# A retention layer with a SwiGLU FFN: the FFN's products from three 12-bit products in two sums, in place of float32 products with Strassen's scheme

## The chip, the cores and the metric

The kernel runs on one NeuronCore of a Trainium2 chip. The metric is the device time of one execution in microseconds (us). Three executions of the kernel before took 707.82, 710.52 and 709.75 us; the median is 709.75 us. TensorE (PE in the profile, PEld for its weight loads) multiplies, VectorE (DVE) and ScalarE (ACT) work on SBUF and PSUM, GpSimd (POOL) works on SBUF alone, and SyncE (SP) issues most DMAs.

## The reference

The attention half is a decayed recurrence over 768 positions, for 4 sequences and 8 heads of 64. Its output, laid out as 3072 tokens of 512 values, goes through a SwiGLU block with a hidden width of 1536.

```python
gamma = 1.0 - 2.0 ** (-5.0 - np.arange(H))
for t in range(S):
    state = gamma * state + k[:, :, t] (x) v[:, :, t]      # outer product, per head
    y[:, :, t] = scale * q[:, :, t] @ state
x = y.transpose(0, 2, 1, 3).reshape(B * S, H * D)          # 3072 x 512
g = x @ w_gate                                             # 512 x 1536
silu = g * (1.0 / (1.0 + np.exp(-g)))
val = x @ w_val                                            # 512 x 1536
return (silu * val) @ w_out                                # 1536 x 512
```

The FFN's weights reach the kernel as float64 numbers, seen as pairs of 32-bit words.

## The kernel before, in words

**Retention.** The recurrence is done in chunks of 128 positions: scores of a chunk, times a mask of decays, times v, plus q times the state carried from the chunk before. `retention` (helpers at L502) does it for two sequences at a time with matmuls of 64 rows; the first segment has older forms (L385, L425, L442, L445). All of it is float32.

**Segments.** The 3072 tokens go through in 4 segments (NSEG) of 6 chunks, so 768 tokens, held as two halves of 384 (TH). A segment is a stage "up" (x times w_gate and w_val, gate, product) and a stage "down" (times w_out). While a segment's down stage runs, the retention matmuls of the next segment are placed between its products (`step`, called after each product, pops them from a list by a table of due places, DUE).

**Strassen.** Every FFN product is one level of Strassen's scheme in Winograd's form, 7 products for 8, and from the second segment on the up stage nests a second level (`up2`). Sums of weight blocks and of token blocks have to be made first: `sums_t` and `sums_u` for the weights, `sums_x`, `sums_2` and `sum_h` for the tokens; and the products have to be joined (L755, ACT, DVE and POOL). Weight sums of the second level, 21 units of 896 KB, are kept in DRAM and read again in each segment through a ring of 6 buffers (`load_unit`).

**The matmuls.** A float32 matmul of the source stands in the trace as two MATMUL records, each with a LDWEIGHTS record. The up stage of the first segment has 168 matmuls of 384 columns (L679), that of each later segment 294 of 192 columns (L790), a down stage 126 of 256 columns (L873 and L883).

**Conversion.** In the first up stage the weights are converted from float64 words to float32 by `convert_a` (ACT: absolute value at L237, sign into a PSUM bank at L241, low word at L244), `convert_b` (DVE: clamp at L254, shift at L256, sign merged at L260) and `convert_c` (POOL: integer add at L269). A block of w_gate with w_val is 128x1024, a block of w_out 128x512. DMAs: L215 for the words, L144 for the converted sums back to DRAM.

**Order.** All orders are written out by hand: every engine runs its instructions in the order in which the source issued them, and waits in that order. L114 loads chunks at the start; `load_side` (L476, L477) loads masks in pieces.

Of the kernel before, what the change touches and what calls it, by code (L numbers as in the profile page):

```python
# [10 lines left out]
F32 = mybir.dt.float32  # L11
I32 = mybir.dt.int32
# [12 lines left out]
L = 3  # L25
TH = L * P
NSEG = B * NCK // (2 * L)
KH = NC // 2
FH = NF // 2
DH = DM // 2  # L30
HT = TH // 2
NQ = NF // 4
NU = 7 * NQ
RING = 6
TA = 3 * P


MASK0, QDEC0, KDEC0, GDEC0 = 0, 2 * NP * P, 3 * NP * P, 3 * NP * P + H
NTAB = GDEC0 + NP


@with_exitstack
def tile_retnet_swiglu(
# [16 lines left out]

# [9 lines left out]
    def place(name, n):  # L90
        return consts.tile([P, n], F32, name=name)

    hsp, midp, loadp, iop = (place(nm, n) for nm, n in (
        ("hsp", 4 * FH * P), ("midp", 6 * TA), ("loadp", 8 * 512), ("iop", 6 * 512)))
    hT = consts.tile([P, NF, 2, TH], F32, name="hT")
    ring = [consts.tile([P, 7 * KH * P], F32, name=f"ring{i}") for i in range(RING)]
    banks = [psum.tile([P, 512], F32, name=f"bank{i}") for i in range(8)]
    turn = {}

    def bank(tag):  # L100


        own = {"s": (4, 5), "y": (6, 7)}[tag]
        turn[tag] = turn.get(tag, -1) + 1
        return banks[own[turn[tag] % len(own)]]


    chunks = {}

    def load_chunk(c, places):  # L110

        for t in places:
            own = chunks.setdefault(c, [])
            nc.sync.dma_start(out=t, in_=(k_t, q_t, v_n, k_n)[len(own)][c])  # L114
            own.append(t)

    def seg_chunks(s):

        p, pos = divmod(s * L, NCK)
        return [(2 * p + i) * NCK + pos + j for j in range(L) for i in range(2)]  # L120

    tab = consts.tile([P, NTAB], F32, name="tab")


    wt = {}
    wot = [consts.tile([P, 7, DH], F32, name=f"wot{j}") for j in range(FH)]
    T3, B22, B12, T1, B11, B21, T2, T4 = 0, 1, 2, 2, 3, 4, 5, 6


    U1, U11, U21, U3, U22, U2, U4 = range(7)  # L130
    unit_b = [kept.tile([P, 7, 2, 4, P], F32, name=f"unitb{q}", tag=f"unitb{q}")
              for q in range(NQ)]
    unit_t = [kept.tile([P, 2, 7, P], F32, name=f"unitt{n}", tag=f"unitt{n}")
              for n in range(NU)]
    PRODUCTS = (1, 5, 6, 2, 7, 3, 4)
    SLOT = {1: B11, 5: T1, 6: T2, 2: B21, 7: T3, 3: B22, 4: T4}

    def new_wt(f):
        wt[f] = ring[f % 4].rearrange("p (a b) -> p a b", a=7)

    def keep_wt(f):

        q, b, h = f // 4, f // 2 % 2, f % 2
        nc.sync.dma_start(out=unit_b[q][:, :, h, ds(2 * b, 2)],  # L144
                          in_=wt[f].rearrange("p a (k f) -> p a k f", k=KH))

    units = {}

    def load_unit(n, whole, slot=None):
        t = ring[n % RING if slot is None else slot]  # L150
        t = t.rearrange("p (h a b) -> p h a b", h=2, a=7)
        if whole:
            nc.sync.dma_start(out=t, in_=unit_t[n])
        else:
            nc.sync.dma_start(out=t[:, :, ds(U11, 4)],
                              in_=unit_b[n // 7][:, SLOT[PRODUCTS[n % 7]]])
        units[n] = t

    def sums_u(n, engine=nc.vector):

        w = units[n]
        sub = engine.tensor_tensor

        def first():
            sub(w[:, :, U1 : U3 + 1 : 3], w[:, :, ds(U3, 2)], w[:, :, U11 : U3 + 1 : 2],
                op=ALU.subtract)

        def last():
            sub(w[:, :, U4], w[:, :, U21], w[:, :, U2], op=ALU.subtract)  # L169
            nc.sync.dma_start(out=unit_t[n], in_=w)  # L170

        return [first,
                lambda: sub(w[:, :, U2], w[:, :, U22], w[:, :, U1], op=ALU.subtract),
                last]

    raw = {}

    def span(piece):  # L180

        kind, a, h = piece
        if kind == "up":
            return wt[a], B22, 4
        return wot[a], (B22, B11)[h], 2

    def load_piece(piece):

        kind, a, h = piece
        if kind == "up":  # L190
            new_wt(a)
            gate, val = (w[:, ts(a, P)].rearrange("(c p) f -> p c f", p=P)
                         for w in (w_gate, w_val))
            parts = [(val[:, ds(KH, KH)], 0), (val[:, ds(0, KH)], 1), (gate, 2)]
        else:
            top, low = (w_out[ts(a + FH * i, P)] for i in range(2))
            parts = ([(low[:, DH:], 0), (top[:, DH:], 1)],
                     [(top[:, :DH], 0), (low[:, :DH], 1)])[h]
        to, slot, n = span(piece)
        to = to[:, ds(slot, n)]  # L200
        if w_gate.dtype != F32:
            t = raw_places[kind].pop(0)
            if kind == "down" or a:
                raw_places[kind].append(t)
            to = raw[piece] = t.bitcast(U32).rearrange("p (a b) -> p a b", a=n)
        for src, i in parts:
            if w_gate.dtype != F32:
                src = src.bitcast(U32)
# [7 lines left out]

# [51 lines left out]
    def sums_t(piece, parts=range(3)):  # L274
# [10 lines left out]
        if kind == "up" and parts[-1] == 2:  # L285
            keep_wt(a)

# [861 lines left out]
```

## Time and profile before

| what | value |
|---|---|
| runs | 707.82, 709.75, 710.52 us |
| span of the profiled execution, first to last instruction | 706.6 us |
| own device time of the profiled execution | not given; the runs' median is 3.15 us over its span |
| granted TensorE clock | 1.000 of full speed |
| PE busy | 691.0 us, 5132 records |
| DVE, ACT, POOL busy | 466.0, 251.5, 240.2 us |
| DMA | 139.92 MB, mean 198 GB/s |

The profile is of one execution. Busy time is the time in which an engine has at least one instruction running; a group's "mean ns" is the length of one record, and PE's records overlap, so the time that a matmul costs is read from how many of them a stretch without gaps holds. "Chain" is the work that ended last, followed back from the last instruction; a stretch of it that says "PE bank L790 x584" is 584 records with nothing between them.

### The profile page before, as it was taken

The page shows a single profiled execution, that of the slowest core. Times are in us where ns is not written, and L with a number is a line of the kernel's source. Part 1 is how long each engine was busy: PE and PEld are TensorE (multiplying, and loading weights), DVE is VectorE, ACT ScalarE, POOL GpSimd, SP SyncE. Part 2 cuts the span into 40 slices and gives each one's busy share as a digit, 9 for nine tenths or more (in the row PEclk, how much of TensorE's full clock was granted, in tenths as well). Part 3 has the DMA queues.
Part 4 walks back from the last instruction along what each step waited for, and adds up shares of the span by engine and source line. Part 5 has one row for each costly group of instructions (what it writes and reads, how often), then busy time and mean ns, then how long its engine had stood idle before and what let it go on. Part 6 is the DMA issues. An engine that isn't in the chain of part 4 may idle for free.

```text
span 706.6 us, 12979 instructions
## 1 busy us (share of the span) xinstructions
PE 691.0 (98%) x5132; PEld 601.3 (85%) x5132; DVE 466.0 (66%) x830; ACT 251.5 (36%) x514; POOL 240.2 (34%) x147
## 2 busy tenths in 40 slices
PE   7998999999999899999999999999999999999998
PEld 7654555578888899998888999998888999999887
DVE  3887998778858987876353675657551666657420
ACT  2658777511333233421322333331222324342000
POOL 0334444403300738280230455474210182644000
PEclk9999999999999999999999999999999999999999
DMA  9798897657999858581570555562291255630010
GB/s 316 261 369 281 284 300 239 176 138 221 354 355 369 316 183 306 206 252 45 188 305 1 186 198 198 194 210 67 84 374 38 86 205 209 209 105 0 24 37 30
DMA packets 63356, 139.92 MB, mean 198 GB/s; under 512 B 6336, under 2 KB 30272, under 8 KB 63296
## 3 DMA queue, kind: packets, MB, share of 16 engines
q1 hardware_dynamic: 59552, 132.81, 55.6%
q10 hardware_dynamic: 3744, 6.29, 2.4%
q8 instruction: 40, 0.66, 0.4%
q14 instruction: 20, 0.16, 0.1%
HBM read 102.51 MB, written 36.57 MB: 197 GB/s over the span
## 4 chain that ended last, share of the span: by engine, by line
PE 83%; DMA 8%; DVE 3%; issue 3%; ACT 2%; POOL 1%; SPq 0%; DVEq 0%; ACTq 0%; POOLq 0%
PE bank L790 38%; PE bank L873 23%; PE bank L679 13%; PE bank L502 4%; PE bank L883 4%; DMA out_dram<-iop 1%; DMA unitt<-ring 1%; DMA loadp<-in_w_gate_dram 1%; DMA hsp<-in_w_gate_dram 1%; DMA hT<-in_v_n_dram 1%; DMA loadp<-in_q_t_dram 1%; DMA ring<-unitb 1%; DMA hT<-in_k_t_dram 1%; DVE ring L169 0%; DVE iop L755 0%
## 5 line engine op out<-in xcount | busy, mean ns | idle before, releaser
L790 PE MATMUL bank<-loadp,ring 128*128 128x192 f32 x720 | 140.6, 327 | 0.7 <-DVE iop L755 0.7
L873 PE MATMUL bank<-wot,hsp 128*128 128x256 f32 x576 | 129.4, 382 | 0.0
L790 PEld LDWEIGHTS bank<-loadp,ring 128*128 128x128 f32 x720 | 120.4, 190 | 2.4 <-DVE iop L755 1.3
L873 PEld LDWEIGHTS bank<-wot,hsp 128*128 128x128 f32 x576 | 108.1, 190 | 16.0 <-issue 1.4
L755 DVE TENSOR_TENSOR iop<-bank,iop 128x384 f32<-128x384 f32 x144 | 79.7, 556 | 50.1 <-PE bank L790 46.8
L790 PE MATMUL bank<-xs,ring 128*128 128x192 f32 x432 | 88.0, 326 | 1.2 <-DVE iop L755 1.2
L755 ACT COPY hsp<-bank 128x384 f32<-128x384 f32 x90 | 42.9, 478 | 102.5 <-PE bank L790 94.0
L825 POOL TENSOR_TENSOR hT<-iop 128x768 f32<-128x768 f32 x36 | 67.1, 1863 | 35.4 <-DVE iop L755 35.4
L755 POOL TENSOR_TENSOR iop<-hsp,midp 128x768 f32<-128x768 f32 x9 | 16.3, 1812 | 174.8 <-ACT hsp L755 140.3
L790 PEld LDWEIGHTS bank<-xs,ring 128*128 128x128 f32 x432 | 73.1, 190 | 1.5 <-DVE iop L755 1.5
L790 PE MATMUL bank<-xT,ring 128*128 128x192 f32 x324 | 66.3, 327 | 0.2 <-DVE midp L755 0.2
L873 PE MATMUL bank<-wot,hT 128*128 128x256 f32 (+1 forms) x300 | 65.9, 373 | 0.5 <-ACT iop L960 0.4
L679 PE MATMUL bank<-xs,ring 128*128 128x384 f32 x192 | 64.7, 488 | 1.1 <-ACT iop L700 0.5
L873 PEld LDWEIGHTS bank<-wot,hT 128*128 128x128 f32 x300 | 54.9, 190 | 8.4 <-DVE iop L948 0.6
L679 PEld LDWEIGHTS bank<-xs,ring 128*128 128x128 f32 x192 | 36.1, 190 | 27.8 <-ACT iop L700 1.1
L790 PE MATMUL bank<-hsp,ring 128*128 128x192 f32 x288 | 56.7, 326 | 0.5 <-ACT hsp L755 0.5
L790 PEld LDWEIGHTS bank<-xT,ring 128*128 128x128 f32 x324 | 54.7, 190 | 1.4 <-DVE iop L755 0.8
L755 DVE TENSOR_TENSOR midp<-bank,midp 128x384 f32<-128x384 f32 x72 | 39.9, 554 | 17.9 <-PE bank L790 14.8
L679 PE MATMUL bank<-xT,ring 128*128 128x384 f32 x144 | 49.8, 489 | 1.8 <-DVE hT L716 1.6
L790 PEld LDWEIGHTS bank<-hsp,ring 128*128 128x128 f32 x288 | 48.4, 190 | 0.8 <-ACT hsp L755 0.8
L944 DVE TENSOR_TENSOR iop<-bank,iop 128x256 f32<-128x256 f32 x12 | 5.1, 424 | 64.7 <-PE bank L873 51.8
L679 PEld LDWEIGHTS bank<-xT,ring 128*128 128x128 f32 x144 | 26.9, 190 | 21.9 <-DVE hT L716 2.2
(152 smaller groups left out, 973.4 us busy)
## 6 DMA issues: line engine op xcount, KB each, us to landing
ring<-unitt SPq DMA_DIRECT2D x50, 896.0 KB, 4.6
unitt<-ring SPq DMA_DIRECT2D x21, 896.0 KB, 6.0
unitb<-ring SPq DMA_DIRECT2D x12, 896.0 KB, 7.0
ring<-unitb SPq DMA_DIRECT2D x21, 512.0 KB, 5.9
out_dram<-iop ACTq DMA_DIRECT2D x23, 256.0 KB, 2.5
loadp<-in_w_val_dram SPq DMA_DIRECT2D x18, 256.0 KB, 4.1
loadp<-in_w_gate_dram SPq DMA_DIRECT2D x9, 512.0 KB, 6.6
midp<-in_w_out_dram SPq DMA_DIRECT2D x12, 256.0 KB, 6.0
```

The lines of the kernel that those rows point to most:

```text
L502: nc.tensor.matmul(o, a, b, start=start, stop=True, skip_group_check=True)
L679: nc.tensor.matmul(o, w[:, slot, k], a[:, k], start=(start and k == 0), stop=(stop and k == KH - 1), skip_group_check=True)
L755: events.append((t, len(events), lambda: fn(*args, **kw)))
L790: nc.tensor.matmul(o[:, h], w[:, h, slot], rhs, start=(start and h == 0), stop=True, skip_group_check=True)
L825: by_block(9.5, 13.5, lambda r: pool(to[:, r], u2[:, r], p5[:, r], op=add))
L873: nc.tensor.matmul(o[:, cols], a[:, k], wot[k][:, slot, cols], start=(start and k == 0), stop=(k == FH - 1), skip_group_check=True)
L883: nc.tensor.matmul(o, a_dn(0, 0, u)[:, k], wot[k][:, B11], start=(k == 0), stop=(k == FH - 1), skip_group_check=True)
L944: tt(ev[0][:, DH:], wb, u2, op=ALU.add)
```

## The change

The Strassen sums, their buffers, the ring of units and the DRAM copies of sums are gone. The kernel has 6 segments (NSEG = NCK) of 512 tokens: one chunk of all four sequences. The first segment's up products stay float32 matmuls, now 8 per block of 128 hidden columns with 512 columns each, straight (`up_first`). All other FFN products (5 up stages, 6 down stages) are made of three matmuls each on operands of the type float32r (R12 in the source), in which both operands have been cut to 12 significant bits: a value a becomes hi (a times CUT, stored as R12), lo (a minus hi) and mid (a combination of both), and the three products hi·hi, lo·lo and mid·mid go into two PSUM sums, that `bring` (ACT) and `joined` (DVE) put together. w_out is converted in the first up stage, split there into its three parts, and stays in SBUF; w_gate and w_val are converted there, kept in DRAM as float32 (512 KB per block, `keep_up`), and read and split again in every later segment (`load_raw`, `up_hi` on ACT, `up_lo` on POOL, `up_mid` on DVE). The hidden values are split in the same way (`h_hi`, `h_lo`, `h_mid`). The instruction order is no longer written as nested loops with places: every call is entered in a list with a planned time, `at(time, function)`, and the list is sorted by it; on each engine the order of the calls is what remains of these times.

The diff, cut to its core. Of the products:

```diff
-            def product(o, slot, rhs, start):                    # up2, 192 columns
-                w = units[n]
-                for h in range(2):
-                    nc.tensor.matmul(o[:, h], w[:, h, slot], rhs,
-                                     start=(start and h == 0), stop=True,
-                                     skip_group_check=True)
...
-            for k in range(FH):                                  # down, 256 columns
-                nc.tensor.matmul(o[:, cols], a[:, k], wot[k][:, slot, cols],
...
+TOK = B * P
+NSEG = NCK
...
+    def up_first(f, g, o):
+        for c in range(NC):
+            nc.tensor.matmul(banks[o], block(made[f % 4], g, c), xr[:, c], start=c == 0,
+                             stop=c == NC - 1, skip_group_check=True)
...
+    def up(x, f, g, part, o):
+        w = w_of[f]
+        for c in range(NC):
+            nc.tensor.matmul(banks[o + (part == 2)], block(w[:, part], g, c), x[:, part, c],
+                             start=c == 0 and part != 1, stop=c == NC - 1 and part != 0,
+                             skip_group_check=True)
...
+    def down(u, j, part, o):
+        h = h_of[u, j]
+        for k in range(FH):
+            nc.tensor.matmul(banks[o + (part == 2)], h[:, part, ts(k, P)],
+                             wo[part][:, FH * j + k],
+                             start=j == k == 0 and part != 1,
+                             stop=j == 1 and k == FH - 1 and part != 0,
+                             skip_group_check=True)
```

Of the splits and joins:

```diff
+    def hi_of(o, a):
+        nc.scalar.activation(o, a, AF.Copy, scale=CUT)
+    def lo_of(o, a, hi, op=pool):
+        op(o, a, f32(hi), op=sub)
+    def mid_of(o, lo, hi):
+        stt(o, f32(lo), -FAR, f32(hi), op0=mul, op1=add)
+    def wo_hi(i):
+        nc.vector.tensor_scalar(wo[0][:, i], down_made(i), CUT, None, op0=mul)
+    def wo_lo(i):
+        lo_of(wo[1][:, i], down_made(i), wo[0][:, i])
+    def wo_mid(i):
+        mid_of(wo[2][:, i], wo[1][:, i], wo[0][:, i])
+    def wo_far(i):
+        nc.gpsimd.tensor_scalar(wo[1][:, i], f32(wo[1][:, i]), FAR, None, op0=mul)
...
+    def bring(i, o):
+        nc.scalar.activation(outs[i], banks[o], AF.Copy, scale=BACK)
+    def joined(i, o, to=None):
+        stt(banks[o + 1] if to is None else to, banks[o + 1], CZ, outs[i], op0=mul, op1=add)
+    def up_gate(f, o):
+        nc.scalar.activation(sg(f), banks[o + 1], AF.Silu)
+    def up_val(f, o):
+        tt(hT[:, f], banks[o + 1], sg(f), op=mul)
```

Of the plan for the start and the first up stage (`convert_abs`, `convert_sign`, `convert_low` are ACT's three steps at 1024 or 512 columns, `convert_clamp`, `convert_shift`, `convert_merge` DVE's, `convert_add` POOL's):

```diff
+    PASS = 0.216
+    UP, HB = 24 * PASS, 18 * PASS
+    ORDER = [(0, 0), (1, 0), (0, 1), (1, 1), (2, 0), (2, 1), (3, 0), (3, 1)]
+    for t, p, w in ((0.0, 0, "k"), (0.1, 0, "q"), (0.4, 0, "v"), (0.5, 1, "k"), (0.6, 1, "q"),
+                    (0.8, 1, "v"), (3.0, 0, "n"), (3.1, 1, "n")):
+        at(t, load, 0, p, w)
+    at(0.2, load_side, 0)
+    at(0.3, load_side, 1)
+    at(0.7, load_up_words, 0)
+    at(0.9, load_up_words, 1)
+    at(2.9, load_tables)
...
+    at(12.6, mix_other, 0, 0, 6)
+    at(12.7, fence, 2)
+    at(13.6, mix_other, 0, 1, 2)
+    for p, o in ((0, 6), (1, 2)):
+        for i in range(2):
+            at(13 + p + 0.1 * i, lambda p=p, i=i, o=o: nc.scalar.copy(
+                xr[:, :, ts(2 * p + i, P)], y_in(o, i)))
+    B0, PERIOD = 16.0, 32 * PASS
+    for f in range(NF):
+        b, o = B0 + PERIOD * f, (2, 4)[f % 2]
+        if f > 1:
+            at(b - 18, load_up_words, f)
+        at(b - 9.4, convert_abs, "up", f)
+        at(b - 9.0, convert_sign, "up", f, sign[f])
+        at(b - 8.6, convert_clamp, "up", f)
+        at(b - 7.8, convert_low, "up", f)
+        at(b - 7.6, convert_shift, "up", f)
+        at(b - 6.8, convert_merge, "up", f, sign[f])
+        at(b - 5.4, convert_add, "up", f)
+        at(b - 0.5, keep_up, f)
+        at(b, up_first, f, 0, o)
+        at(b + PERIOD / 2, up_first, f, 1, o + 1)
+        at(b + PERIOD / 2 + 0.2, up_first_gate, f, o)
+        at(b + PERIOD + 0.2, up_first_val, f, o + 1)
+        at(b - 6, load_down_words, f)
+        own = (sign[f][0],)
+        at(b + 0.5, convert_abs, "down", f)
+        at(b + 0.6, convert_sign, "down", f, own)
+        at(b + 0.9, convert_clamp, "down", f)
+        at(b + 1.2, convert_low, "down", f)
+        at(b + 1.7, convert_shift, "down", f)
+        at(b + 2.0, convert_merge, "down", f, own)
+        at(b + 2.8, convert_add, "down", f)
+        at(b + 4.2, wo_hi, f)
+        at(b + 4.8, wo_lo, f)
+        at(b + 6.2, wo_mid, f)
+        at(b + 6.8, wo_far, f)
+    for p in range(2):
+        for i in range(2):
+            at(B0 + PERIOD - 3 + p, scale_k, p, i)
```

Of the plan for the segments (t is the planned start of a down product group of 18 matmuls, b that of an up block of 24):

```diff
+            at(t - 5.5, h_hi, u, j)
+            at(t - 4.6, h_lo, u, j)
+            at(t - 2.5, h_mid, u, j)
+            for part in range(3):
+                at(t + part * HB / 3, down, u, j, part, o)
...
+                at(b - 13, load_raw, f)
+                at(b - 7.5, up_hi, f)
+                at(b - 6.5, up_lo, f)
+                at(b - 3.9, up_mid, f)
+                for g in range(2):
+                    c = b + g * UP / 2
+                    for part in range(3):
+                        at(c + part * UP / 6, lambda *a: up(new["x"], *a), f, g, part, o + 2 * g)
+                    at(c + UP / 3 + 0.2, bring, g, o + 2 * g)
+                    at(c + UP / 2 + 0.2, joined, g, o + 2 * g)
+                    at(c + UP / 2 + 1.0, (up_gate, up_val)[g], f, o + 2 * g)
```

The retention of a segment's pairs is placed between the down product groups as before: scores after the 1st and 5th group, the sums after the 3rd and 4th, the 6th and 7th. It keeps its float32 matmuls of 64 rows.

## The prediction, on record before the result

> **What bounds the kernel now.** I read the page's busy shares and granted clock first:
>
> ```profile
> PE 691.0 (98%) x5132; PEld 601.3 (85%) x5132; DVE 466.0 (66%) x830; ACT 251.5 (36%) x514; POOL 240.2 (34%) x147
> ...
> PEclk9999999999999999999999999999999999999999
> ```
>
> PE is busy 98% of the span, at full clock in all slices. Busy alone doesn't prove a bound, so the page's chain comes next:
>
> ```profile
> PE 83%; DMA 8%; DVE 3%; issue 3%; ACT 2%; POOL 1%; SPq 0%; DVEq 0%; ACTq 0%; POOLq 0%
> PE bank L790 38%; PE bank L873 23%; PE bank L679 13%; PE bank L502 4%; PE bank L883 4%; DMA out_dram<-iop 1%; DMA unitt<-ring 1%; DMA loadp<-in_w_gate_dram 1%; DMA hsp<-in_w_gate_dram 1%; DMA hT<-in_v_n_dram 1%; DMA loadp<-in_q_t_dram 1%; DMA ring<-unitb 1%; DMA hT<-in_k_t_dram 1%; DVE ring L169 0%; DVE iop L755 0%
> ```
>
> 83% of the path is matmuls, nearly all of the FFN (L790, L873, L679). The chain in order of time (start us, duration us, what) then gives the true cost of a matmul, since these pieces have no gap:
>
> ```profile
> 69.14 72.48 PE bank L679 x224
> ...
> 321.92 1.50 PE bank L502 x64
> ...
> 386.66 95.09 PE bank L790 x584
> ...
> 653.67 31.08 PE bank L873 x144
> ```
>
> 72.48/224 = 323.6 ns per record of 384 columns (L679); 95.09/584 = 162.8 ns for 192 (L790); 31.08/144 = 215.8 ns for 256 (L873). All are two clocks of 2.4 GHz per column (320, 160, 213.3 ns) plus 2.5 to 3.6 ns, and a source matmul is two such records: four passes. The retention costs 26 ns per record: its seven pieces in the down stage from 322 us hold 544 records in 14.14 us. The windows view of one L790 stage, fields PE, PEld, DVE, ACT, POOL busy:
>
> ```profile
> 386.66:481.75 95.09, 95.09 (x585) 94.85 (x585) 60.42 (x112) 33.46 (x65) 48.53 (x27) 1.00 0.55 187
> ```
>
> Here the other engines have room (DVE 60 of 95). In the first up stage they have less: DVE 63.46, ACT 52.77 of 72.48 us.
>
> **What the Trainium skill says.** "FP8 and Floating Point Precision", TensorE Precision Notes: true FP32 takes four passes, "FP32 reduced precision" reads 4 bytes and truncates to FP22, which I read as one pass. The trace agrees on the four; no run here shows the other. "TensorE: Matmul & The Clock Gate", "Wait — 56ns, not 53.3ns?": a warm matmul costs N/2.4 + about 2.5 ns, 215.7 at 512; the three costs above agree, with 2N for N. Same page, "LDWEIGHTS": 128 columns load in about 107 ns. The trace's records last 190 ns, and yet matmuls 162.8 ns apart were not held up, so a load hides behind a 216 ns matmul. "GPSIMD Engine Reference", 3.1: a tight loop takes 768 ns for 512 elements, two inputs cost more; used below for `wo_far`.
>
> **The change, part by part.**
>
> *FFN matmuls.* Removed: 336 records x 323.6 ns, 1764 x 162.8, 1008 x 215.8 = 108.7 + 287.2 + 217.5 = 613.4 us. Added: 96 float32 matmuls of 512 columns, two records each at 2 x 213.3 + 2.7 = 429.4 ns: 82.4 us. And 5 x 12 x 24 = 1440 float32r matmuls (up) and 6 x 144 = 864 (down). Their price is unknown here: at least 215.9 ns (one pass), at most 429.4 (as slow per record as float32; a further record each would give 858.8). I take 215.9: 310.9 + 186.5 = 497.4 us. Sum 579.8, so 33.6 us less work.
>
> *Retention in later segments.* The same kind of matmuls: 10 pairs of sequences x 160 records and 8 x 32 for states = 1856 x 26 ns = 48.3 us on PE.
>
> *Later stages beside PE.* Per up block of 24 x 215.9 = 5.18 us: DVE one 1024-wide split (1.2, by L861's 0.99 for 768), two joins and a product of 512 (0.68 each, as L260): 3.2. ACT a 1024 copy (1.16, L237) and three of 512 (0.6): 3.0. POOL one 1024 subtraction: 2.4. DMA 512 KB, 101 GB/s. Per down group of 3.89 us: POOL 1.86, ACT 1.5, DVE 1.6. All below PE's, and the split for block f+2 is started while f runs. The DMAs removed here were larger (50 loads of 896 KB and 21 of 512 KB, 21 stores of 896 KB; now 60 loads of 512 KB). Two waits are new in the down stage: PE's later half of the retention sums waits for a tiny DVE read of the earlier half (`fence`), with a product group of 3.9 us between them that covers DVE's queue; and ACT's split of the hidden values waits for DVE's last product of the up stage, needed only after two groups, 7.8 us later; behind it in ACT stands the next `bring`, as late. Cost: nothing while PE covers it; I allow 2 us for handovers. Without that cover DVE would be next, 2 us below PE.
>
> *Start.* SP's queue is passed by `load_side`, 16 small DMAs ahead of the weight words. The trace shows what one costs to issue:
>
> ```profile
> 151.67 0.47 SPq L476 DMA_DIRECT2D kept_vk<-in_decays_dram  x1
> 152.23 0.63 SPq L477 DMA_DIRECT2D kept_vk<-in_decays_dram  x1
> ```
>
> The next starts 0.56 us after the first; all eight of that call took from 151.67 to 156.80, 0.64 us each. So: k, q to 2.6 us; 16 masks to 12.9; v, the second k and q to 16.5; the first block's words issued by 18.5 and landed at 22.3 (256 KB took 4.1 us). Behind that, in each engine's order: abs 1.16; clamp 0.69; two mask products 1.0; shift 0.69; merge 1.28; four mask products 2.0 (DVE); two retention steps on PE 1.7; ACT's two copies of x 1.1, abs, sign and two more copies 3.4, low word 1.16. That is 36.5 us for the second block's add on POOL, and about 35.5 for the first matmul of `up_first`. Before, the first FFN matmul ran at 31.4 us (chain).
>
> *First up stage.* PE needs 16 x 429.4 = 6.87 us per block. Read DVE's and POOL's orders after the change, however: POOL has add(up f+1), add(w_out f), wo_lo(f), wo_far(f), add(up f+2); DVE has wo_hi(f), clamp(f+2), wo_mid(f), shift(f+2), merge(f+2). wo_hi waits for POOL's add of w_out f, wo_lo for wo_hi, wo_mid for wo_lo, and the next block's merge stands in DVE's queue behind wo_mid, while its add waits for the merge. That is a closed loop, with the times of before:
>
> ```profile
> L269 POOL TENSOR_TENSOR ring<-ring,loadp 128x1024 int32<-128x1024 int32 x8 | 19.3, 2410 | 41.4 <-PE bank L679 15.4 <-ACT ring L237 5.3 <-issue 5.2
> ...
> L260 DVE SCALAR_TENSOR_TENSOR ring<-bank,ring 128x512 uint32<-128x512 uint32 x24 | 15.4, 683 | 0.7 <-ACT bank L693 0.5
> ...
> L269 POOL TENSOR_TENSOR wot<-wot,midp 128x512 int32<-128x512 int32 x6 | 7.8, 1296 | 0.0
> ...
> L254 DVE TENSOR_SCALAR wot<-wot 128x512 f32<-128x512 f32 x12 | 5.0, 420 | 0.0
> ```
>
> add 1024 2.38 (start to start), add 512 1.29, wo_hi 0.42 (as L254's 512), wo_lo 1.28 (POOL 512, L399), wo_mid 0.62, shift 0.66, merge 1.28 (two back to back), five hand-overs of 0.05: 8.2 us per block against PE's 6.87. Before, DVE waited for POOL's add only 1.7 us in all (L284, same view), and PE stayed full. wo_far is not in the loop while it takes under 1.94 us (shift and merge); by the skill's 0.77 as estimate and L399's 1.28 it does. So PE idles 1.3 us per block. The DMA queue isn't the bound at that pace: 1 MB of up words, 0.5 of w_out's and 0.5 kept per 8.2 us are 256 GB/s, and this stage moved 249 before (windows view). Four `scale_k` (1.3 us each on POOL) come in the first turn: the adds begin at 36.5, w_out's ends at 40.2, scale_k to 42.8, wo_lo to 44.1, scale_k to 46.7, wo_far 47.8, and block 2 is added at 50.2. The nine blocks after it: 9 x 8.2 = 73.8, to 124.0. The last block's matmuls: 130.9. POOL then still has w_out's last pieces ahead of the first `h_lo`: 1.5 us wait.
>
> *End.* Last join 0.7, DMA issue 0.34, a 256 KB store 2.5: 3.5 us.
>
> *Sum.* 132.4 + 186.5 + 310.9 + 48.3 + 2.0 + 3.5 = 683.6 us of span, against 706.6. The runs' median lies 3.15 us over the span of the profiled execution, whose own time isn't given: 686.8 us. So of 33.6 us less FFN work some 10 are lost to the loop and the later start, net of the stalls that the start has now.
>
> **Rivals.**
> 1. *The loop doesn't bind* (DVE gets ahead, or the pieces overlap more): blocks at 6.87 us: 9 x 1.33 = 12 us less: 675 us. For it: DVE and POOL each have only about 6.2 us of work per block. Against: the fixed order.
> 2. *Waits in the later stages.* 10 up and down handovers and 60 raw loads; the loop of two buffers is a landing (5.9 us for 512 KB), a copy 1.16, a subtraction 2.4: 9.5 us per two blocks, against 10.4 of PE. If landings take 7.5 us or more, each pair costs 0.7 us, 30 pairs 20 us: 707 us. For it: the narrow margin; against: DMA is far less loaded there (101 GB/s against 198).
> 3. *Slower: the float32r matmul costs more than I take it to.* One mechanism, in 2304 matmuls of the later stages, from reading 4-byte columns at half rate or a weight load that doesn't hide. Break-even: (709.75 - 686.8)/2304 = 10 ns more, so 226 ns each. At 429.4 ns: 686.8 + 2304 x 0.2135 = 1179 us. For it: float32's record does take two clocks per column. Against: the skill's four passes explain those as two passes.
> 4. *It isn't done*: the type makes no difference and four passes stay, 858.8 ns: 2168 us.
>
> **How the numbers follow.** My forecast (loop binding, one pass): 0.55, 680 to 695 us with the start uncertain by 4 and the loop by 0.4 us x 9. Rival 1: 0.13, 668 to 680. Rival 2: 0.19, 695 to 715. Rival 3: 0.12. Rival 4: 0.01. A measurement of this kernel can tell about 0.5% from no change, which is 3.5 us. Faster by that (below 706.2): 0.55 + 0.13 + 0.12 = 0.80; within: 0.05; slower: 0.02 + 0.12 + 0.01 = 0.15. The range for 8 in 10 takes in the forecast, nearly all of rival 1 and two thirds of rival 2: 670 to 706.
>
> **What would show it.** A gapless stretch of up matmuls in a later stage with 216 ns per record shows the pass; 430 shows rival 3. Starts of the 1024-wide POOL adds 8.2 us apart between 50 and 124 us, with PE idle just over 1 us per block, show the loop; 6.9 us apart, rival 1. The first FFN matmul at 35 us, the first float32r one at 131. PE idle behind ACT's copies that wait for a DMA in up stages: rival 2. Wrong would be above all the price of the pass; then the start, where small issues and one DVE queue decide.

## The result, and the profile after

The kernel after takes 764.62 us (764.03 to 765.50, 4 runs), the kernel before 709.14 beside it (707.82 to 710.52, 4 runs): ratio 1.079, interval 1.077 to 1.081. The change makes the kernel slower; 686.8 us and a range of 670 to 706 were forecast. The profiled execution took 764.62 us, with a span of 762.8.

The page of the kernel after, busy shares and slices of 19 us:

```profile
PE 697.3 (91%) x4672; PEld 527.6 (69%) x4672; DVE 443.6 (58%) x573; ACT 307.5 (40%) x469; POOL 350.5 (46%) x180
...
PE   1479777789999999999999999999999999999998
...
PEclk8589999899999999999999999999999999999999
```

PE was 98% busy before and is 91% now. Beside the start, the hole is in the fifth to ninth slice, 76 to 172 us: the first up stage. The chain of the same page:

```profile
PE 53%; issue 15%; DVE 14%; POOL 10%; DMA 4%; SPq 2%; ACT 2%; ACTq 0%; POOLq 0%; DVEq 0%
```

PE's share of the path fell from 83% to 53%; DVE and POOL now hold a quarter of it. Two gapless pieces of the chain in order of time (start, duration, what) give the price of the new products:

```profile
327.10 63.76 PE bank L430 x280
...
725.36 33.74 PE bank L449 x144
```

63.76/280 = 227.7 ns for an up product and 33.74/144 = 234.3 for a down product (from the start of one to the start of the next, inside the stages: 226.8 and 234.2), not 215.9. One turn of the first up stage, that is one block, in the timeline of GpSimd (start us, duration us, operation; in brackets the idle time before and what ended it, "issue" where the profile shows nothing):

```profile
97.40 2.37 POOL L339 TENSOR_TENSOR first<-first,words 128x1024 int32<-128x1024 int32 x1 [0.27 <-DVE first L334]
101.45 1.30 POOL L339 TENSOR_TENSOR raw<-raw,words 128x512 int32<-128x512 int32 x1 [1.68 <-issue]
103.28 1.65 POOL L350 TENSOR_TENSOR wo<-raw,wo 128x512 fp32r<-128x512 f32 x1 [0.54 <-DVE wo L356]
105.75 1.86 POOL L365 TENSOR_SCALAR wo<-wo 128x512 fp32r<-128x512 f32 x1 [0.82 <-DVE wo L353]
107.89 2.37 POOL L339 TENSOR_TENSOR first<-first,words 128x1024 int32<-128x1024 int32 x1 [0.27 <-DVE first L334]
```

and VectorE in the same turn:

```profile
97.68 2.37 DVE L324 TENSOR_SCALAR raw<-raw 128x512 f32<-128x512 f32 x1
100.09 0.43 DVE L328 TENSOR_SCALAR raw<-raw 128x512 uint32<-128x512 uint32 x1
100.62 0.69 DVE L334 SCALAR_TENSOR_TENSOR raw<-bank,raw 128x512 uint32<-128x512 uint32 x1
102.78 0.43 DVE L356 TENSOR_SCALAR wo<-raw 128x512 fp32r<-128x512 f32 x1 [1.46 <-POOL raw L339]
103.12 0.69 DVE L324 TENSOR_SCALAR first<-first 128x1024 f32<-128x1024 f32 x1
104.97 0.69 DVE L353 SCALAR_TENSOR_TENSOR wo<-wo,wo 128x512 fp32r<-128x512 f32 x1 [1.16 <-POOL wo L350]
105.58 0.69 DVE L328 TENSOR_SCALAR first<-first 128x1024 uint32<-128x1024 uint32 x1
106.37 1.29 DVE L334 SCALAR_TENSOR_TENSOR first<-bank,first 128x512 uint32<-128x512 uint32 x2
```

The loop of the prediction is there: add, add, wo_hi, wo_lo, wo_mid, shift, merge, and the next add, each waiting for the one before. But it takes 10.49 us and not 8.2. The clamp of w_out (L324, 128x512) lasts 2.37 us where the kernel before showed 0.42 for the same form; it ends at 100.05, just behind GpSimd's add (99.77). Behind it stand shift and merge (100.09, 100.62), and while they run GpSimd waits 1.68 us, in "issue". In the same way GpSimd's wo_lo (103.28), which starts while VectorE's clamp of the next up block runs (103.12 to 103.81), lasts 1.65 us; the one wo_lo of this kernel with no SBUF-only operation of VectorE beside it, at 155.70, lasts 1.27.

The granted clock was 0.90 on the mean between 40.6 and 161.3 us, but it doesn't set this pace: PE's 16 matmul records of a block took 7.13 us in some turns and 8.5 to 8.8 in others, the starts of the adds were 10.44 to 10.51 us apart all the same, and PE waited 1.65 to 3.35 us for each.

The span by stretches, from the first record of each stage's products; "best" is the last experiment:

| stretch, us | predicted | after | best |
|---|---|---|---|
| start to the first FFN matmul | 35.5 | 40.6 | 35.3 |
| from there to the first down product | 96.9 | 120.7 | 91.7 |
| six down stages with the retention | 234.8 | 264.3 | 259.0 |
| five up stages | 310.9 | 333.5 | 328.0 |
| handovers, allowed | 2.0 | (inside) | (inside) |
| end | 3.5 | 3.7 | 3.7 |
| span | 683.6 | 762.8 | 717.7 |

### The profile page after: what moved, and what is told of

It reads as the page before. It is cut to its first block, busy times and chain, and to the rows that moved or that the text cites. A ratio compares the mean times of both kernels' runs of the same rounds, so it can differ in the third digit from the quotient of the medians.

```text
span 762.8 us, 11810 instructions
## 1 busy us (share of the span) xinstructions
PE 697.3 (91%) x4672; PEld 527.6 (69%) x4672; DVE 443.6 (58%) x573; ACT 307.5 (40%) x469; POOL 350.5 (46%) x180
## 4 chain that ended last, share of the span: by engine, by line
PE 53%; issue 15%; DVE 14%; POOL 10%; DMA 4%; SPq 2%; ACT 2%; ACTq 0%; POOLq 0%; DVEq 0%
PE bank L430 42%; PE bank L449 10%; POOL item L350 4%; DVE item L353 3%; DVE raw L324 3%; POOL wo L350 2%; DMA words<-in_w_val_dram 2%; POOL raw L339 2%; POOL n L239 2%; DVE first L334 1%; PE bank L154 1%; DVE wo L353 1%; DVE x L278 1%; DVE x L274 1%; DVE first L328 1%
## 5 line engine op out<-in xcount | busy, mean ns | idle before, releaser
L430 PE MATMUL bank<-x,item 128*128 128x512 f32 x1440 | 328.8, 390 | 5.6 <-DVE x L278 5.6
L430 PEld LDWEIGHTS bank<-x,item 128*128 128x128 f32 x1440 | 269.9, 188 | 63.6 <-DVE x L278 7.7
L350 POOL TENSOR_TENSOR item<-raw,item 128x1024 fp32r<-128x1024 f32 x60 | 144.6, 2410 | 165.8 <-DVE bank L438 114.0
L449 PE MATMUL bank<-wo,item 128*128 128x512 f32 x864 | 212.1, 400 | 3.9 <-DVE raw L334 1.9
L449 PEld LDWEIGHTS bank<-wo,item 128*128 128x128 f32 x864 | 160.0, 188 | 45.7 <-issue 4.8
L435 ACT ACTIVATE outs<-bank 128x512 f32<-128x512 f32 x144 | 86.0, 597 | 244.3 <-PE bank L430 133.7
L350 POOL TENSOR_TENSOR item<-hT,item 128x768 fp32r<-128x768 f32 x48 | 92.5, 1929 | 157.4 <-ACT item L347 156.4
L353 DVE SCALAR_TENSOR_TENSOR item<-item 128x1024 fp32r<-128x1024 f32 (+1 forms) x108 | 133.1, 1237 | 50.0 <-POOL item L350 50.0
L438 DVE SCALAR_TENSOR_TENSOR bank<-bank,outs 128x512 f32<-128x512 f32 x120 | 83.9, 699 | 125.3 <-PE bank L430 118.1
L418 PE MATMUL bank<-first 128*128 128x512 f32 x192 | 94.6, 652 | 22.5 <-POOL first L339 18.9
L441 ACT ACTIVATE tmp<-bank 128x512 f32<-128x512 f32 x60 | 35.8, 597 | 18.3 <-DVE bank L438 14.0
L278 DVE TENSOR_TENSOR x<-x 128x512 fp32r<-128x512 f32 x20 | 30.2, 1516 | 0.0
L154 PEld LDWEIGHTS bank<-q,k 64*64 64x64 f32 x704 | 17.9, 141 | 14.8 <-issue 8.8
```

The source lines that it names most:

```text
L154: nc.tensor.matmul(o, a, b, start=start, stop=True, skip_group_check=True)
L278: op(x[:, 2, :, c], f32(x[:, 0, :, c]), f32(x[:, 1, :, c]), op=sub)
L350: op(o, a, f32(hi), op=sub)
L353: stt(o, f32(lo), -FAR, f32(hi), op0=mul, op1=add)
L418: nc.tensor.matmul(banks[o], block(made[f % 4], g, c), xr[:, c], start=c == 0, stop=c == NC - 1, skip_group_check=True)
L430: nc.tensor.matmul(banks[o + (part == 2)], block(w[:, part], g, c), x[:, part, c], start=c == 0 and part != 1, stop=c == NC - 1 and part != 0,
```

## The experiments

Theory at the start: the 79 us (span of 762.8 against 683.6 predicted) are four separate losses, each a price or an order that can be tried alone: the price of a float32r matmul, a hold of VectorE by GpSimd in the first stage (VectorE's operation ends only after the one that GpSimd is running), SP's issue at the start, and waits behind `fence`. Rivals: the float32r price is an effect of its surroundings in the kernel; the loop is set by the order or by GpSimd's load and not by a hold; the start is set by transfers.

### price_of_r12: float32r matmuls alone

24 matmuls of each kind one after the other on one PE, from loaded tiles; among them:

```diff
+    def weight_off_64():
+        for i in range(24):
+            nc.tensor.matmul(banks[1], sta[:, ds(128 * (i % 12) + 16, 128)],
+                             mov[:, ts(i % 6, 512)], start=True, stop=True, ...)
```

> This kernel leaves the whole computation out; it only runs blocks of 24 matmuls (12 for float32) into one PSUM bank, with operands of float32r, bfloat16 and float32, at several sizes and places in SBUF. The changed kernel showed 226.7 ns per float32r matmul of 512 columns in the up stage, where both operands start 32 bytes past a multiple of 64, and 234.3 ns in the down stage, where only the stationary one does. Theory A (place of the operands): operands on multiples of 64 give 216 ns, as the float32 ones of the kernel before had no such loss; the stationary operand alone at +32 bytes gives 234, both at +32 give 227. Theory B (the type): float32r costs 13 ns more than the 213.3 ns of its columns wherever the operands lie, so 227 in all blocks, 173 at 384 and 120 at 256 columns. Theory C (weight load not hidden): the block with one and the same weight is no faster, but 384 and 256 columns come out well above 173 and 120. bfloat16 should give 216 in all theories, float32 two records of 429.

Chain in order of time: L92, L96, L100 are float32r with 512, 384 and 256 columns; L128, L132, L136 have the moving operand, the weights, or both 64 bytes further on, L112 and L148 both 16 and both 80 bytes; L164 is bfloat16, L168 float32 (two records a matmul):

```profile
16.41 5.44 PE bank L92 x24
21.85 4.18 PE bank L96 x24
26.03 2.87 PE bank L100 x24
...
40.06 5.52 PE bank L112 x24
...
62.26 5.49 PE bank L128 x24
67.75 5.60 PE bank L132 x24
73.35 5.46 PE bank L136 x24
...
89.93 5.59 PE bank L148 x24
...
111.85 5.20 PE bank L164 x24
117.04 10.31 PE bank L168 x24
```

226.7, 174 and 120 ns: from 256 to 512 columns 107 ns come on, so 0.42 ns a column, one clock at 2.4 GHz, and some 13 ns besides at all three widths. bfloat16 needs 216.7, float32 429.6 per record. So it is one pass, as predicted, and 11 ns dearer than the 2.6 ns over the columns that I had taken from other types; what these 11 ns are stays open. Where the weights lie 64 bytes further on than the moving operand, 7 ns come on top (5.60/24 = 233.3). With both 64 bytes on it is 227.5, but with both 16 or both 80 bytes on 230.0 and 232.9, so that equal places are not the whole rule.

### align and align512: what the down products lose besides

```diff
-    small = place("small", 2 * H + NP)
+    small = place("small", 32)        # align; 128 in align512
```

A wider tile moves everything behind it, x and the items, but not w_out's parts.

> The tile `small` is declared 32 columns wide in place of 20 (nothing more is written into it), so that every tile after it, x and the items among them, starts on a multiple of 64 bytes in its partition, as the w_out parts already do. Theory A (the extra of the down products over the up products comes from the places of the two operands: weights from an item at 32 mod 64, moving from w_out at 0 mod 64): starts of consecutive down matmuls come 226.7 ns apart where they came 234.3, the up ones stay at 226.7; 864 x 7.6 ns = 6.6 us, total about 758. Theory B (the down products are slower because their weights were just written by three engines, or because they change bank between the second and third pass): 234 ns stays, total about 764.6.

Measured: 762.01 us (761.55 to 764.04), 232.7 ns. Same place mod 64 isn't enough.

> `small` is 128 columns wide: x and the items then start at 128 bytes above a multiple of 512, where the w_out parts start too. In the kernel after, the two operands of an up product lie at the same place mod 512 (both at 224) and take 226.7 ns, those of a down product do not (224 and 128) and take 234.3; in align they lay at 256 and 128 and took 231 on the mean. Theory A (the full speed of a float32r product needs stationary and moving operand at the same place mod 512 bytes): the down products come 226.7 ns apart, total about 758 (864 x 7.6 = 6.6 us less than 764.6). Theory B (what the down products lose is set by something else than their place): 230 to 234 ns, total 761 to 765.

Measured: 760.74 us (760.22 to 762.17; ratio to before 1.074, 1.070 to 1.077), 228.0 ns on the mean, and the last down stage, 33.74 us above, is

```profile
722.05 32.65 PE bank L449 x144
```

32.65/144 = 226.7. So the 7.5 ns come from the operands' places, and vanish in this kernel when these are the same mod 512 bytes. That this is enough is shown only for multiples of 32 bytes: both operands 16 or 80 bytes on were dear in price_of_r12, though at the same place mod 512. Both runs fell short of the total expected (2.6 and 3.9 us instead of 6.6). The down stages became 4.3 us shorter in align512. Why places matter is not shown.

### hold_price: VectorE beside GpSimd, alone

> The reference's computation is left out: only VectorE operations of eight kinds on 128x512 float32, six of each, once with GpSimd idle and once while GpSimd runs 36 adds of 128x1024 (2.38 us each) one after the other with no dependency between the engines. Theory A (a VectorE operation whose operands are all in SBUF is held until GpSimd's running operation ends; one with an operand in PSUM is not): clamp, scale, two-input and copy of SBUF to SBUF take 0.4 to 0.7 us alone and about 2.4 us under the adds, while the three kinds with one PSUM operand take the same 0.6 to 0.7 us in both. Theory B (only the faster forms of VectorE, the one-input ones at 0.43 us, are held): the two-input SBUF forms stay at 0.7 us. Theory C (no hold, the stretch in the kernel was a wait for data): nothing changes under the adds.

Of this kernel's eight kinds of VectorE operation, three are shown: `tensor_scalar` SBUF to SBUF (L86), two SBUF inputs (L89), one PSUM input (L95). Timeline of VectorE, first with GpSimd idle, then under its adds; six operations each:

```profile
6.24 2.73 DVE L86 TENSOR_SCALAR d<-a 128x512 f32<-128x512 f32 x6
8.89 4.31 DVE L89 SCALAR_TENSOR_TENSOR e<-a,b 128x512 f32<-128x512 f32 x6
...
20.12 4.31 DVE L95 TENSOR_SCALAR d<-bank 128x512 f32<-128x512 f32 x6
...
44.02 12.16 DVE L86 TENSOR_SCALAR d<-a 128x512 f32<-128x512 f32 x6
56.10 13.87 DVE L89 SCALAR_TENSOR_TENSOR e<-a,b 128x512 f32<-128x512 f32 x6
...
95.87 4.30 DVE L95 TENSOR_SCALAR d<-bank 128x512 f32<-128x512 f32 x6
```

No operation depends on the other engine here, and still a SBUF operation of 0.43 us takes 2.00 (mean of one), one with two SBUF inputs 2.26 instead of 0.69, about as long as one add of GpSimd (1.9 to 2.2 us here); with a PSUM operand it takes 0.69 in both. Theory A holds, B and C fall. It is what the Trainium skill says ("SBUF — State Buffer", "Who interferes with whom": VectorE in a two-port mode or with two SBUF inputs contends with GpSimd, and whoever is first holds the shared ports for its whole instruction). That the forms of 0.43 us run in a two-port mode is my reading, no run shows it. I had not applied that section to the loop.

### clamp_psum: the hold taken out of the loop

```diff
-        nc.scalar.activation(d, f32(hi), AF.Abs)
+        nc.scalar.activation(d if kind == "up" else banks[sign[n][1]], f32(hi), AF.Abs)
...
-        d = parts_of(kind, n)[0]
+        d = parts_of(kind, n)[0] if kind == "up" else banks[sign[n][1]]
```

The shift reads that PSUM bank too, and writes to SBUF.

> Only the w_out blocks' absolute values go into a spare PSUM bank, and clamp and shift read them from there, so that DVE's two operations don't read SBUF. Theory 1 (DVE's SBUF-to-SBUF clamp is held until POOL's running 1024-wide add ends: it took 2.04 us on the mean here and 0.42 before): the period of a block in the first stage goes from 10.49 to about 8.8 us, since the 1.68 us that POOL waits for the merged w_out vanish; 12 blocks are about 19 us, so 746 us. Theory 2 (the clamp is long because it waits for its own input from ACT): no change, 764 us. Theory 3 (POOL's own work sets the period): no change, or a little more, as the PSUM forms are slower.

Measured: 749.82 us (748.67, 750.97). GpSimd's 128x1024 adds start 9.07 us apart (10.49 in the kernel after). The timelines of GpSimd and VectorE in this kernel:

```profile
99.06 2.38 POOL L340 TENSOR_TENSOR first<-first,words 128x1024 int32<-128x1024 int32 x1 [0.27 <-DVE first L335]
101.69 1.29 POOL L340 TENSOR_TENSOR raw<-raw,words 128x512 int32<-128x512 int32 x1 [0.26 <-issue]
```

```profile
99.35 0.69 DVE L324 TENSOR_SCALAR bank<-bank 128x512 f32<-128x512 f32 x1
```

The clamp under the running add takes 0.69 us, and the wait of 1.68 is 0.26. The hold of the clamp is worth 9 x 1.41 = 12.7 of the 14.8 us gained.

### split_later and mid_late: order against hold

```diff
-        at(b + 4.2, wo_hi, f)          # 4.8 wo_lo, 6.2 wo_mid, 6.8 wo_far
+        at(b + 7.2, wo_hi, f)          # 8.8 wo_lo, 9.7 wo_mid, 10.6 wo_far
```

> Only the planned times of the four steps that split w_out are later (7.2, 8.8, 9.7, 10.6 us after the block's start instead of 4.2, 4.8, 6.2, 6.8), so that the next block's merge stands ahead of them in DVE's queue and its add ahead of them in POOL's. Theory 1 (a closed loop through the two queues sets 10.49 us per block): the loop is cut, POOL's work of 2.37 + 1.29 + 1.65 + 1.86 = 7.2 us or PE's 6.87 us is left; 7.4 us per block, 11 blocks are 34 us: 730 us. Theory 3 (POOL is held by DVE whenever both work on SBUF, whatever the order): under 10 us of gain, above 754 us.

Measured: 760.49 us (760.03, 760.96), adds 10.14 us apart. Now wo_hi, 0.43 us of work, stands beside the add and takes 2.38, and everything behind it is late. In `mid_late`, far_on_act (below) with wo_mid moved to 7.6, it is wo_mid:

> far_on_act with VectorE's third w_out operation (wo_mid) planned at 7.6 in place of 6.2, behind the shift and the merge of the next block's words in VectorE's order. far_on_act left GpSimd idle 2.9 us before each add, and the adds as far apart as before (9.07 us): the loop then ran from the end of GpSimd's wo_lo through VectorE's wo_mid, shift (0.68) and merge (1.29) to the next add. Theory A (that order is the loop): the adds come 7.4 to 8.2 us apart (the shift is still held by the running wo_lo, the merge still follows it), total 749 - 9 x 1.2 = 738. Theory B (something else holds the 9.07 us, for instance ACT's abs or the words' landing): adds 8.9 us apart or more, total 748 to 750.

Measured: 763.76 us (763.28 to 766.45), adds 10.84 us apart instead of the 7.4 to 8.2 of theory A. The timeline of both engines:

```profile
96.33 2.37 POOL L340 TENSOR_TENSOR first<-first,words 128x1024 int32<-128x1024 int32 x1 [2.17 <-DVE first L335]
96.63 2.63 DVE L354 SCALAR_TENSOR_TENSOR wo<-wo,wo 128x512 fp32r<-128x512 f32 x1
```

Two reorderings that ought to shorten the chain only exchanged which operation is held; what GpSimd runs beside the moved operation was missing from both expectations. split_later came out in the range of its theory 3 (above 754 us).

### far_on_act: was it GpSimd's load?

```diff
-        nc.gpsimd.tensor_scalar(wo[1][:, i], f32(wo[1][:, i]), FAR, None, op0=mul)
+        nc.scalar.activation(wo[1][:, i], f32(wo[1][:, i]), AF.Copy, scale=FAR)
...
-        at(b + 6.8, wo_far, f)
+        at(b + 8.6, wo_far, f)
```

It contains clamp_psum.

> clamp_psum, and the third w_out operation of GpSimd (x FAR, 1.86 us a block) done by ACT, planned at 8.6 instead of 6.8. Theory A (what is left of the loop after the hold is gone is the chain through GpSimd's and VectorE's orders, 9.07 us, of which 1.86 + 0.27 + 0.81 stand between GpSimd's last w_out operation and its next add): GpSimd's adds come 6.9 to 7.4 us apart, the rate of TensorE's 16 float32 matmuls (6.87 us) or just above, and the total falls by 9 x 1.8 = 16 us from 749.8 to about 733. Rival (ACT, 5.5 us a block, becomes the bound with 1.2 us more and its own waits, or VectorE is held by other GpSimd operations): adds 8 us apart or more, total 740 to 750.

Measured: 749.30 us (748.78 to 750.30), adds 9.07 us apart: nothing. GpSimd is idle for 2.9 us where wo_far stood. The rival's numbers are met, but neither its cause nor theory A is right: ACT isn't late, and VectorE isn't held. The adds wait for VectorE's wo_mid, shift and merge, which take as long as wo_far did beside them. The releaser "0.27 <-DVE first L334" in the timeline of the kernel after had said so.

### up_early: the merge ahead of wo_mid

```diff
-        at(b - 7.6, convert_shift, "up", f)
-        at(b - 6.8, convert_merge, "up", f, sign[f])
+        at(b - 7.6 - 1.2 * e, convert_shift, "up", f)        # e = 3 from f = 2 on
+        at(b - 6.8 - 0.8 * e, convert_merge, "up", f, sign[f])
```

abs, sign, clamp and low are moved by e; it contains far_on_act. In this kernel the sign bits of the next up block overwrite those of a w_out block before these are merged.

> far_on_act with the abs, sign, clamp, low and shift of the next up words planned 3 to 3.6 us earlier and their merge 2.4 us earlier, so that they come before wo_mid, in the time in which VectorE waits for GpSimd. Theory A (the loop is GpSimd to VectorE and back, and only its order): with the merge done before wo_lo ends, the loop is add 2.39 + 0.24 + 1.29 + 0.54 + wo_lo 1.65 + 0.25 = 6.4 us, so TensorE's 6.87 us take over: adds 6.9 to 7.5 us apart, the nine blocks 9 x 1.8 = 16 us shorter than in far_on_act, total about 733. Theory B (VectorE's SBUF operations are held by GpSimd's wherever they are put, and ACT's by the banks): adds 8 to 9 us apart, total 740 to 749.

Measured: 746.08 us (744.09 to 748.38). For four turns the adds come 7.45 us apart, as theory A has it; then 10.5 and 14.0, with GpSimd waiting for VectorE's merge of w_out's words, whose loads stood behind those of segment 1 in SP's queue. The loop was order and hold; a transfer was next.

### masks_act: the start

```diff
-                nc.sync.dma_start(out=side[g][half[m], i, : 2 * P], in_=cols[half[0]])
+                nc.scalar.dma_start(out=side[g][half[m], i, : 2 * P], in_=cols[half[0]])
...
```

> The 16 DMAs of the decay masks are issued from ACT's queue in place of SP's, where they stood ahead of the words of block 0. Theory A (SP's issue of the start is the path to the first FFN matmul): the words of block 0 are issued some 9 us earlier, the first FFN matmul comes 5 to 9 us before 40.6, and, since the nine-block loop only shifts, the total falls by as much: about 757. Theory B (the landing of the words, 7.5 us, is set by all the transfers of the start sharing the DMA engines, and the first FFN matmul by the mixing of segment 0 besides): first FFN matmul within 2 us of 40.6, total 762 to 766.

Measured: 759.55 us (758.82 to 760.18), 5.1 less. The first FFN matmul comes at 35.2 us instead of 40.6. The first words are issued, and ACT's first step on them starts, in the kernel after and then in masks_act at

```profile
17.50 1.29 SPq L292 DMA_DIRECT2D words<-in_w_gate_dram  x2
...
27.79 1.12 ACT L311 ACTIVATE first<-words 128x1024 f32<-128x1024 f32 x1 [25.58 <-DMA words<-in_w_val_dram]
```

```profile
13.61 1.59 SPq L292 DMA_DIRECT2D words<-in_w_gate_dram  x2
...
21.36 1.12 ACT L311 ACTIVATE first<-words 128x1024 f32<-128x1024 f32 x1 [19.15 <-DMA words<-in_w_val_dram]
```

The issue is only 3.9 us earlier, not 9: SP's queue now stands still between issues, for 2.3 us before 6.35 and for 2.0 before 13.61, why is open. ACT starts 6.4 us earlier, so the words also landed some 2.5 us sooner after their issue. Theory A has the path right and its size too large; that the landing changes with what else is in transit speaks for a part of theory B.

### fence_later: the new wait of the down stage

```diff
-                at(t + 0.02, fence, 6)
+                at(t + 0.5, fence, 6)
```

> Only the fence between the two halves of the retention sums is planned 0.5 us later, behind the join of the output tile in DVE's queue instead of ahead of it. Theory 1 (fence waits for the retention sums on PE, the join behind it is late by that, the store's issue on ACT waits for the join, the next split stands behind the store on ACT, and so the x of the next segment is late): PE's idle of about 2 us at each of five entries to an up stage goes to under 0.5, so 6 to 8 us less, 757 us. Theory 2 (x is late because DVE and POOL slow each other down at that place, splits of 1024 and 768 at once): at most 2 us less.

Measured: 755.53 us (755.52, 755.55). The kernel after enters each up stage with a stall; the costliest groups give for L430 an idle time of 5.6 us, all for `x_mid` (L278). In fence_later the chain has the stage in one piece:

```profile
209.66 65.28 PE bank L430 x288
```

65.28/288 = 226.7: no stall. The up stages lose 6.2 us of their 333.5, the down stages 1.8; the remaining 1.0 of the 9.1 us is the start, which this edit doesn't touch. VectorE's tiny reads of the retention's bank had stood ahead of its joins, the joins ahead of the store's issue in ACT's queue, and that ahead of the next split.

### all4 and best: do the losses add up?

`all4` is far_on_act, align, masks_act and fence_later in one.

> far_on_act, align, masks_act and fence_later in one kernel. If the losses lie one after the other on TensorE's path they add: 764.6 - 31 (far_on_act) - 6.6 (align) - 7 (masks_act) - 9 (fence_later) = 711. If they overlap (an earlier start that only waits at the first w_out block, a fence whose place matters only with the old down times), the total is 716 to 735. Below the kernel before (709) is expected with a chance of 0.25.

Measured: 735.16 us (734.33 to 736.66). From far_on_act's 749.3, the three others gave alone 2.6 + 5.1 + 9.1 = 16.8, so 732.5: the losses add but for 2.7 us. What the expectation of 711 lacked is far_on_act, which gave 15.3 instead of 31.

`best` adds the order of up_early (2.5 us earlier, its sign behind the merge of w_out's), align512's place, and

```diff
-            t0 = end - 40
+            t0 = end - (40 if s else 12)
```

> all4 with align512's place instead of align's, the next block's conversion 2.5 us earlier as in up_early (with its sign planned behind the merge of the w_out words), and the loads of segment 1 issued 28 us later, so that they no longer stand between the words of the last blocks. Theory A (the loop was order and hold, and the losses lie one after the other): GpSimd's adds 7.2 to 7.8 us apart over all blocks, the first stage 9 x 1.5 = 13.5 us shorter than in all4 (735.2), the down products 3 us less: about 719. Theory B (words now land too late, since their buffers come free no sooner): adds 8.5 us apart or more, total 725 to 735. Neither is below 709: what would be left are float32r products 11 us dearer per thousand than predicted and the retention of segments 1 to 5.

Measured: 718.99 us (717.49 to 719.48; ratio to before 1.014, 1.011 to 1.017). GpSimd in one turn of the first stage, and VectorE's wo_mid at its end:

```profile
86.88 2.93 POOL L340 TENSOR_TENSOR first<-first,words 128x1024 int32<-128x1024 int32 x1
90.75 1.30 POOL L340 TENSOR_TENSOR raw<-raw,words 128x512 int32<-128x512 int32 x1 [0.94 <-issue]
93.02 1.28 POOL L351 TENSOR_TENSOR wo<-raw,wo 128x512 fp32r<-128x512 f32 x1 [0.96 <-DVE wo L357]
94.35 2.93 POOL L340 TENSOR_TENSOR first<-first,words 128x1024 int32<-128x1024 int32 x1
...
94.33 0.69 DVE L354 SCALAR_TENSOR_TENSOR wo<-wo,wo 128x512 fp32r<-128x512 f32 x1 [0.20 <-POOL wo L351]
```

The adds are 7.45 to 7.47 us apart over the last seven turns, theory A. The add itself is 2.93 now, since wo_mid with its two SBUF inputs starts 0.02 us before it; and wo_lo, with no SBUF-only operation of VectorE beside it, is down from 1.65 to 1.28. The hold works both ways. best beats the kernel after by 45.6 us and not the kernel before.

## Why the prediction was wrong

**FFN matmuls.** "I take 215.9" failed: 226.8 ns (up) and 234.2 (down). That is 1440 x 10.9 + 864 x 18.3 = 15.7 + 15.8 = 31.5 us. Mechanism right (one pass), size wrong; rival 3's break-even of 226 ns was reached by this term alone. Rival 3's number came true, but not its first reason: the columns go at one clock each, not two. A fixed part of the weight load that doesn't hide isn't ruled out. Its chance of 0.12 was too small for a price that no row of the profile showed: 2304 uses make 10 ns into 23 us.

**First up stage.** The loop was the right mechanism; its 8.2 us failed with 10.49. Of the 2.29 missing, the hold of the clamp gives 1.42 (1.68, less the 0.26 that stays in clamp_psum), the hold of wo_lo by VectorE's clamp 0.37 (1.65 for L399's 1.28), and 0.5 are handovers. Over nine blocks 20.5 us. `wo_far`, 1.86 us for an estimated 0.77 to 1.28 (1.49 where no SBUF-only operation of VectorE runs at its start), stayed just beside the loop, as the rule "under 1.94" had it; far_on_act bears this out. Apart from wo_far's, the durations used were right for operations alone, and wrong for an operation beside the other engine.

**Start.** 35.5 became 40.6. The words were all issued by 20.1, not 18.5, and ACT waited for their landing until 27.79, not 22.3 (18.5 and the 4.1 taken for a landing would be 22.6). The orders behind that took what the prediction had. That the landing is longer because many transfers of the start are under way at once is likely: in masks_act, with the masks in another queue, it was some 2.5 us shorter; it wasn't tried by itself. masks_act gave the 5 us back.

**Retention.** 1856 records at 26 ns, 48.3 us, were 56.1, so 30 ns each (from the start of the last product before a piece to the start of the first after it, less one product). Why a record takes 30 ns and not 26 is open. Besides, the first product after a piece is followed by the next only after 338 ns where 234 is usual, 105 ns more; the same 338 ns stand after stalls with no retention in them (at 163.12 us). This is read from the trace, and was not tried by itself.

**Waits of the later stages.** "Nothing while PE covers it; I allow 2 us" failed: `fence` costs 8.0 us in these stages. The cover of 3.9 us was there for PE's next step, but the reads stand ahead of work of later groups in VectorE's queue and, through it, in ACT's. The first down stage lost some 4 us more to its splits (49.7 us against 45.9). Rival 2's raw loads didn't bind: they land in 3.2 us by the page. The prediction's list of removed DMAs leaves out 12 stores of 896 KB; nothing was built on it.

**Sum.** Start 5.1, first stage 23.8, down 29.5 (15.8 price, 7.8 retention, 5.9 stalls with the 338 ns after each pause), up with its handovers 20.6 (15.7 price), end 0.2: 79.2 us, the difference of the spans. Two terms carry two thirds of it: the price, 31.5 us, and the loop, 20.5. In best, the start and the first stage are back at or under the prediction; what it has over the prediction elsewhere, 39 us, is 26 of price (1440 x 10.8 and 864 x 11.8 ns), 8 of retention and 5 of stalls.

## What to carry to other kernels

A price that multiplies by thousands must be bounded by its break-even before anything else; if that lies within a few per cent of the assumed value and no row shows the operation, the forecast's sign is open. When GpSimd is given work on a loop, go through VectorE's operations that can fall beside it: of the eight kinds in hold_price, those with only SBUF operands ended only with GpSimd's running operation, and those with an operand in PSUM were free of it. Look at it from the other side too: GpSimd's operation that starts behind such a one of VectorE is held in its turn. And moving an operation is predicted only when it is said what the other engine runs at the new place.

## What was not expected of the hardware

- A float32r matmul costs 0.42 ns a column and some 13 ns more (226.7, 174 and 120 ns for 512, 384 and 256 columns), bfloat16 216.7 at 512.
- The places of its two operands cost it up to 7.5 ns more: 234.2 in the down stages, 228.0 in align512 with both at the same place mod 512 bytes; but 230.0 and 232.9 in price_of_r12 with both 16 or both 80 bytes on.
- SBUF-only work on VectorE lengthens GpSimd's operation that starts behind it, too: the 128x1024 add from 2.37 to 2.93 us in best behind a two-input form, the 128x512 subtraction from 1.27 to 1.65 in the kernel after behind a one-input form. Back to back, in hold_price, the add goes from 1.89 to 2.22 beside two-input forms.
- GpSimd's `tensor_scalar` of 128x512 float32 into float32r takes 1.49 us with no such operation at its start, more than its two-input subtraction (1.27).
